# Halving and reordering the weight loads of a two-part attention kernel, with a new search of its order

## The chip, the cores and the metric

The kernel runs on one core of a Trainium2 chip. Its time is the device time of one execution in microseconds (us). TensorE (PE) does matmuls; its weight loads are shown as PEld. VectorE (DVE), ScalarE (ACT) and GpSimd (POOL) work on tiles. SyncE (SP) and POOL issue most DMAs here, ACT a few. Each engine works through its own queue in order.

## The reference, cut to what matters

Two attentions over the same input `x` (2048 tokens of 576 numbers, bfloat16) are mixed by a gate.

```python
g = sigmoid((x * gate_w).sum(-1))
# A: recurrent over 64 segments of 32 tokens, 32 heads of 128
for s in range(64):
    h = concat([mem, xs])                    # 8 memory rows and 32 tokens
    q, k, v = h @ Wq, h @ Wk, h @ Wv         # 576 -> 4096 each
    o = softmax(mask(q @ k.T) * scale) @ v
    o = o @ Wo                               # 4096 -> 576
    mem = o[:8]; outs.append(o[8:])
# B: plain attention over all 2048 tokens, 32 heads of 18
b = softmax(qB @ kB.T * scale) @ vB @ wo
out = g * a + (1 - g) * b
```

A's segments depend on each other through `mem`. B is independent of A until the last line.

## The kernel before

**Opening.** `x` is loaded in 16 tiles and transposed into `xT` (operations `xt`, evictions `xe`). B's projections follow: `pq` for queries and keys (five blocks of 128 columns, each in four stretches of 512 tokens; number of the kind, block, stretch), `pv` for values (two halves in 16 blocks). Their evictions `pe` and `ve` are, in order of creation, the list `beats`; the numbers in `WV_AT`, `WQ_AT`, `WK_AT` and `XT_AT` are places in it. The results go to DRAM (`ps`, `vs`) and come back by head in rings of tiles (`lq`, `lk`, `lv`). `gate` makes the gate's sums with 80 matmuls of one column.

**Weights of A.** `load_weights` loads each of `Wq`, `Wk` and `Wv` in four row chunks of 1152 KB on POOL's queue: one DMA for 128 rows (`wq_m` and so on) and two for the 16 rows left over (`wq_t`). `Wo` (`wo`) is loaded in four loads of eight heads each, also 1152 KB. `behind` paces such a load: a mark (`mk...`, a memset of one element by VectorE, after a given beat) overwrites a corner of the target, so the load on POOL must wait for it:

```python
mark = add(f"mk{name}", "DVE", 0.07, lambda e: nc.vector.memset(corner(), 0.0), [beat, *deps], prio=0.05)
op = add(name, "POOL", 0.6 * n, fn, [mark, *deps], prio=0.15, kb=kb)
```

The beats of `wo`'s loads are evictions `le0...` of the look-ahead units below.

**Look-ahead units.** The last 8 tokens of each segment are independent of `mem`'s way through the sums, so their projections are made ahead for 16 segments at once. Unit `la{q}.{kind}.{b}` (kind 0 queries, 1 keys, 2 values; b from 0 to 7) is made on TensorE in four or five parts, evicted to one of three `vl` buffers (`le`) and stored to DRAM (`ls`, into `qkd` or `vld`); `ll`, `lw` and `pl` bring it to a segment. Group q = 0 is made in the opening, the other three between the segments. `xs` stores `xT` to `xtd`.

**Recurrence.** `open` releases the opening's tiles. For each segment s, projections `Q0`, `Q1`, `K0`, `K1`, `V0`, `V1` run in quarter tiles (`pvv`), are evicted to `tm` (`eQ`, `eK`, `eV`), queries and keys are transposed by DMA on SP (`tt`) and copied to `qk` (`ct`). Then come scores `ph0`, `ph1` (tile `psh`), the exponential, sums `sm`, reciprocal `rc`, broadcast `bc`, product `nm`, values `po`, copies `co`, the output product `op` (tile `acc`), the sum `oc`, the fold `fo` (tile `pw`) and the VectorE operation `ph{s}`, which writes the new memory rows into `ht`.

**B's attention.** It is cut into 512 visits, each of four score matmuls (`sb`, `sp`), two exponentials on ScalarE and four value matmuls (`ob`). Some 48 run ahead of the first segment; the rest are tied to the segments' progress. After the last segment come B's output projection and the mix (`po` on line 1719).

**The order.** All operations are handed to `Plan`, which knows estimated durations, buffers and DMA lanes and lays out the program's instructions by a list schedule: the kernel's code order does not set it. `transfer` estimates a DMA's landing from a total rate of 300 GB/s. In gaps that it foresees on TensorE it places fillers (`warm`, matmuls of zeros into `ob`). `TURNS` holds one number for each segment and one for the opening; from it `factor` draws multipliers on the priorities of the kinds of operations, which `turn` sets at every segment's start. Another number gives another order of the same operations.

Of the kernel before, what the change touches and what calls it, by code (L numbers as in the profile page):

```python
# [54 lines left out]
]  # L55
RANK = dict(RANKS[0])
TURNS = [
    7952103, 9687964, 5516313, 4619848, 2331426, 9781478, 6767540, 9438387, 4494518, 2665133, 7827388,
    8977164, 1226615, 2691511, 8161648, 3391998, 7299576, 7499803, 5912477, 3941991, 2592632, 3325584,
    1612500, 5268309, 5100667, 9966380, 8690923, 9452778, 8585440, 8557057, 6500948, 6810124, 3017308,  # L60
    4090786, 5458572, 5723550, 5859185, 4641056, 9435998, 2730178, 9332617, 891581, 8429124, 2926893, 2493124,
    3284586, 4758985, 9564957, 2868796, 4844339, 2132632, 1055938, 8169318, 6049240, 2872012, 2408005,
    9273239, 5457756, 9293065, 1220648, 3952921, 2300746, 1937382, 5055776, 6803238,
]
FACTORS = (0.02, 0.1, 0.25, 0.4, 0.55, 0.7, 0.85, 1.0, 1.2, 1.5, 1.9, 2.4, 3.0, 4.0, 6.0, 10.0)
KNOBS = ("switch", "near", "early", "wait", "gap", "cool")
# [17 lines left out]
def kind_of(name):  # L84
    if re.match(r"(sb|ob|ex|ey)\d+\.", name):
        return name[:2]
    if re.match(r"l[ae]\d", name):
        return name[:2] + ("v" if name.split(".")[1] == "2" else "q")
    m = re.match(r"([a-zA-Z]+\d?)\.\d+(?:\.\d+)?$", name) or re.match(r"([a-zA-Z]{2})\d+$", name)
    return m.group(1) if m else "x"  # L90
# [20 lines left out]
class Plan:  # L111
# [36 lines left out]
    def transfer(self, op):  # L148

        wait, after = (0.6, 0.5) if op.end < self.CROWDED[1] else (0.9, 1.0)  # L150
        step = (op.end - op.start) / op.dmas
        for j in range(op.dmas):
            issued = op.start + (j + 1) * step
            self.moved = max(self.moved, issued + wait) + op.kb / op.dmas / 300.0
            self.lanes.append(max(self.moved + after, self.lanes[-1]))
        self.lanes = self.lanes[-self.LANES:]
        op.tail = self.lanes[-1] - op.end
# [13 lines left out]
    def add(  # L171
        self, name, engs, dur, fn, deps=(), prio=5.0, mode=None, take=(), give=(), tail=0.0, dmas=0, kb=0.0,
        use=None, pairs=4, alt=None, waits=0.0,
    ):
        op = Op(name, engs, dur, fn, deps, prio, mode, take, give, tail)
        op.dmas, op.kb = dmas, kb
        op.pairs, op.alt, op.form, op.waits = pairs, alt, mode, waits
        op.kind = self.kinds.setdefault(kind_of(name), len(self.kinds))
        op.use = self.ARRAY.get(mode) if use is None else use
        op.seq = len(self.ops)  # L180
        op.slots = {}
        self.ops.append(op)
        return op
# [19 lines left out]
    def run(self):  # L203
# [20 lines left out]
        while len(order) < n + extra:  # L224
# [3 lines left out]
            for e in free:  # L228
                b = best[e]
# [5 lines left out]
            est, op = best[pick]  # L235
            if pick == "PE" and open_ and self.warm is not None:
                for m in ("col", "full"):
# [6 lines left out]
                    w = Op("warm", "PE", self.WARM, self.warm[m], [], 9.0, m, (), (), 0.0)  # L244
# [39 lines left out]
            if op.dmas and pick == "ACT" and op.prio < 0.05:  # L284
                op.tail = 2.0
            elif op.kb and pick == "POOL":
                self.moved = max(self.moved, op.end + 0.6) + op.kb / 300.0
                op.tail = 2.2 + op.kb / 250.0 if op.dmas else self.moved + 1.0 - op.end
            elif op.dmas:
                self.transfer(op)  # L290
                dirty.add("SP")
# [85 lines left out]
def kernel(  # L377
# [15 lines left out]
    nc = tc.nc  # L393
    P = nc.NUM_PARTITIONS
# [16 lines left out]
    NF = 4  # L411
    RW = Dm // NF
    TR = RW - P
    TL = NF * TR
    HD = H * Dh
    WB = HD // NF
# [14 lines left out]
    plan = Plan()  # L431
# [30 lines left out]
    for jj in range(2):  # L462
        nc.vector.memset(bsel[64 * jj:64 * jj + 64, jj:jj + 1], 1.0)
    nc.gpsimd.affine_select(
        out=veil[0:64, M:L], in_=veil[0:64, M:L], pattern=[[1, seg]],
# [3 lines left out]
        out=veil[0:64, 0:M], in_=veil[0:64, 0:M], pattern=[[0, M]],  # L469
        compare_op=ALU.is_gt, fill=-30000.0, base=L, channel_multiplier=-1,  # L470
    )
    for j in range(4):
# [3 lines left out]
        out=keep[:, NF + 1:NF + 2], in0=keep[:, NF:NF + 1], scalar1=-1.0, scalar2=1.0, op0=ALU.mult, op1=ALU.add  # L476
# [49 lines left out]
    def bank(shape, dt, name, k=0):  # L526
        return ps_a.tile(shape, dt, name=name, tag=f"pb{plan.slot('pb', k)}")
# [42 lines left out]
    def rows(t, c):  # L570
        return t[RW * c:RW * c + P, :]
# [84 lines left out]

    wbl = [*wbt, *wbq.values()]
    beats, weight_loads, paced = [], {}, []
    WV_AT, WQ_AT, WK_AT = (1, 5, 25, 29), (33, 37, 41, 45), (49, 53, 57, 60)
    XT_AT = (63, 64, 66, 67)  # L660

    def behind(name, beat, corner, n, fn, deps, kb):

        mark = add(f"mk{name}", "DVE", 0.07, lambda e: nc.vector.memset(corner(), 0.0), [beat, *deps], prio=0.05)
        op = add(name, "POOL", 0.6 * n, fn, [mark, *deps], prio=0.15, kb=kb)
        paced.append(op)
        return op

    def load_weights(w, src, name, at):
        w2 = src.rearrange("d h e -> d (h e)")  # L670
        weight_loads[name] = []
        for c in range(NF):
            def load_w(e, c=c):
                nc.gpsimd.dma_start(
                    out=w[0][:, :, c, :], in_=rows(w2, c).rearrange("p (b f) -> p b f", f=WB)
                )
                for two in range(2):
                    o = 32 * c + TR * two
                    nc.gpsimd.dma_start(
                        out=w[1][o:o + TR, :],  # L680
                        in_=w2[RW * c + P:RW * c + RW, two * (HD // 2):(two + 1) * (HD // 2)],
                    )

            weight_loads[name].append(behind(f"{name}{c}", at[c], lambda c=c: w[0][0:1, 0, c, 0:1], 3, load_w, [], 1152))

    def load_gw(e):
        for c in range(NF):
# [7 lines left out]
    def store_xt(q):  # L695
# [4 lines left out]

        deps = [beats[XT_AT[q]]] + [o for n in range(4 * q, 4 * q + 4) for o in xdone[n][:1]]
        return add(f"xs{q}", "SP", 0.4, fn, deps, prio=3.0, dmas=1, kb=655)
# [212 lines left out]
    for gq in range(GB * NQC):  # L915
# [3 lines left out]
        for kb in range(NKB):  # L919
            c = 4 * g + kb // KC  # L920
            o = (kb % KC) * P
# [176 lines left out]
    opened = {}  # L1098
# [21 lines left out]

    opening = add("open", "POOL", 4.0, open_rest, b_work + early + paced, prio=0.5)

    wo_loads = []
    for q in range(4):
        def load_wo(e, q=q):
            nc.gpsimd.dma_start(out=opened["wo"][:, 8 * q:8 * q + 8, :], in_=A_Wo[8 * q:8 * q + 8].rearrange("h e d -> e h d"))

        wo_loads.append(behind(
            f"wo{q}", [o for o in plan.ops if o.name.startswith("le0.")][2 + 5 * q],
            lambda q=q: opened["wo"][0:1, 8 * q, 0:1], 1, load_wo, [opening], 1152,  # L1130
        ))

    def load_m0(e):
        m0 = opened["ot"][:, :, :].rearrange("p h t -> p (h t)")[:, 0:Dm]
# [47 lines left out]
    def out_pieces(name, o_of, t0, hf, state, first, last, prio, deps, take, halves=None, wide=False):  # L1182
        def piece(lo):
            def fn(e):
                if state.get("acc") is None:
                    state["acc"] = bank([P, 2 * RW if wide else RW], FP32, "acc")
                acc, o, wo = state["acc"], o_of(), opened["wo"]
                for s_ in range(lo, lo + 4):
                    slot = hf * 16 + s_
                    h = (s_ // 4) * 8 + 4 * hf + s_ % 4  # L1190
                    for j in range(2 if wide else 4):
                        q = 2 * (s_ % 2) + j if wide else j
                        n, d = (2 * RW, 2 * RW * j) if wide else (RW, RW * SL[j])
                        nc.tensor.matmul(  # L1194
                            acc[32 * q:32 * q + 32, :], lhsT=o[:, slot, t0:t0 + CT], rhs=wo[:, h, d:d + n],
                            start=(first and s_ == (s_ % 2 if wide else 0)), stop=(last and s_ == (14 + s_ % 2 if wide else 15)),
                            tile_position=(0, 32 * q), skip_group_check=True,
                        )
            return fn

        op = None
        for k in range(4):
            d = [*(deps if op is None else [op]), *(halves[k // 2] if halves else ())]
            op = add(
                f"{name}{k}", "PE", 0.243 if wide else 4 * 0.0625, piece(4 * k), d, prio=prio, mode="col",
                take=take if k == 0 else (), pairs=8 if wide else 16,
            )
            state.setdefault("op0", op)
        return op
# [32 lines left out]
    for s in range(n_seg):  # L1242
# [122 lines left out]
        ots = []  # L1365
        mids = {}
        for hf in range(2):
# [141 lines left out]
            for jj in range(2):  # L1509
# [10 lines left out]
                ))  # L1520
            acc_state = {}
            mids[hf] = out_pieces(
                f"op{hf}.{s}.", lambda: opened["ot"], 0, hf, acc_state, True, True, RANK[f"op{hf}"],
                wo_loads, ("pb",), [[o] for o in ots[2 * hf:2 * hf + 2]], wide=not hf,
            )
            if hf == 0:
                first_half = acc_state
# [223 lines left out]
    ahead, behind = RANK["ahead"], RANK["behind"]  # L1751
    share = (NB - ahead - behind) / n_seg
    for i, vi in enumerate(order):
        if i >= ahead:
            k = min(int(8 * (i - ahead) / share), 8 * n_seg - 1)
# [40 lines left out]
```

## Time and profile before

| what | value |
|---|---|
| median of 3 runs | 1420.84 us (1417.83 to 1429.57) |
| the profiled execution's own time | 1421.8 us |
| its span | 1420.0 us, 74484 instructions |
| PE busy | 1345.2 us (95%) |
| ACT busy | 1091.4 us (77%) |
| DVE busy | 848.2 us (60%) |
| POOL busy | 535.4 us (38%) |
| moved by DMA | 130.73 MB, mean 92 GB/s |

The span is what the profiler saw from the first instruction to the last. Busy time is summed by engine; a busy TensorE is one with matmuls in flight, with modelled ends. A line such as L1312 is a line of the kernel; where a helper makes the call (L540, L538), the tile's name tells which operation it is. In brackets after a timeline row stands the idle time of the engine before it and what ended it. The granted clock is the share of full clock that TensorE got.

### The profile page before, as it was taken

Reading aid. Unit: us, or ns where it says so; the run is one execution under the profiler, and the core shown is the slowest. Engines: PE = TensorE matmul, PEld = TensorE weight load, DVE = VectorE, ACT = ScalarE, POOL = GpSimd, SP = SyncE. Lnnn points to the kernel's source line nnn. Section 1 sums busy time; section 2 is a strip of 40 time slices with the busy share of each in tenths; the row PEclk is TensorE's granted clock in tenths of the full one; section 3 lists DMA queues with packets and bytes.
Section 4 is the critical chain, followed back from the end, with each engine's and each line's share of the span. In section 5 each row is a group of like instructions: output and inputs, shape, how many; then the busy total and the mean of one; then the engine's idle time right before and its main releaser. Section 6 shows DMA issues by size and latency. Waiting matters only on the chain. (4 is left out here: it accounts for less than half of the span.)

```text
span 1420.0 us, 74484 instructions
## 1 busy us (share of the span) xinstructions
PE 1345.2 (95%) x33172; PEld 720.4 (51%) x33184; DVE 848.2 (60%) x2019; ACT 1091.4 (77%) x1277; POOL 535.4 (38%) x1162
## 2 busy tenths in 40 slices
PE   7999899999999999999999999999999999999998
PEld 4555344555554545555555544555554545444545
DVE  4443466665565566656666655656656665665566
ACT  3477688888887787887887888787778788887884
POOL 7352154334532346332543425333354324521310
PEclk9999999999999999999999999999999999999999
DMA  8787544333433344333433334333335333333335
GB/s 251 253 314 220 131 87 75 64 68 69 82 62 64 60 79 76 76 61 65 85 67 70 69 66 76 68 62 69 65 80 89 60 54 59 72 56 53 56 81 169
DMA packets 343997, 130.73 MB, mean 92 GB/s; under 512 B 296495, under 2 KB 330023, under 8 KB 343675
## 3 DMA queue, kind: packets, MB, share of 16 engines
q1 hardware_dynamic: 315155, 80.47, 29.2%
q0 software_dynamic: 26368, 43.31, 11.4%
q8 instruction: 259, 4.24, 1.3%
q10 hardware_dynamic: 2152, 2.19, 0.5%
q14 instruction: 63, 0.52, 0.1%
HBM read 52.74 MB, written 31.12 MB: 59 GB/s over the span
## 5 line engine op out<-in xcount | busy, mean ns | idle before, releaser
L941 ACT ACTIVATE etb<-sb 128x1536 bf16<-128x1536 f32 x512 | 743.5, 1452 | 227.5 <-PE sp L932 153.0
L540 DVE CAST tm<-pvv 128x512 bf16<-128x512 f32 x358 | 246.3, 688 | 230.3 <-PE pvv L1312 228.3
L945 ACT ACTIVATE etb<-sp 128x512 bf16<-128x512 f32 x512 | 305.0, 596 | 4.8 <-PE sp L932 4.8
L1312 PEld LDWEIGHTS <-ht 128*32 128x32 bf16 x7680 | 202.8, 96 | 196.2 <-issue 21.6
L932 PE MATMUL sb<-qch,kch 32*128 32x512 bf16 x1536 | 201.8, 386 | 3.2 <-ACT etb L941 1.8
L932 PE MATMUL sp<-qch,kch 32*128 32x512 bf16 x512 | 197.6, 386 | 7.6 <-DVE vl L540 5.8
L955 PE MATMUL ob<-etb,vch 128*32 128x512 bf16 x2048 | 201.9, 387 | 0.3 <-issue 0.3
L1194 PE MATMUL acc<-wo,ot 128*32 128x288 bf16 (+1 forms) x6144 | 165.7, 248 | 7.3 <-issue 3.6
L1312 PE MATMUL pvv<-wq_m,ht 128*32 128x512 bf16 x2048 | 142.1, 380 | 3.9 <-DVE ht L1559 1.5
L1312 PE MATMUL pvv<-wv_m,ht 128*32 128x512 bf16 x2048 | 141.7, 380 | 0.3 <-DVE tm L540 0.2
L1312 PE MATMUL pvv<-wk_m,ht 128*32 128x512 bf16 x2048 | 140.5, 380 | 0.1
L1194 PEld LDWEIGHTS <-ot 128*32 128x32 bf16 x6144 | 112.7, 97 | 47.0 <-DVE ot L540 17.7
L540 DVE CAST ot<-pso 128x320 bf16<-128x320 f32 x200 | 91.6, 484 | 58.3 <-PE pso L1500 57.3
L932 PEld LDWEIGHTS <-kch 32*128 32x128 bf16 x2048 | 54.5, 91 | 137.0 <-issue 121.7
L1411 DVE COPY qk<-tt 128x512 bf16<-128x512 bf16 x256 | 79.9, 314 | 54.5 <-DMA tt<-tm 51.2
L1261 POOL COPY ht<-xg 128x96 bf16<-128x96 bf16 x64 | 17.7, 277 | 236.8 <-PE pvv L1312 230.5
L955 PEld LDWEIGHTS <-vch 128*32 128x32 bf16 x2048 | 53.6, 94 | 73.5 <-issue 62.5
L851 POOL DMA_DIRECT2D qch<-qtd x120 | 61.7, 521 | 68.3 <-PE sp L932 64.6
L851 POOL DMA_DIRECT2D otd<-stage x124 | 62.8, 513 | 65.0 <-DVE stage L998 38.6
L540 DVE CAST vl<-pv 128x512 bf16<-128x512 f32 x84 | 57.2, 685 | 38.8 <-PE pv L1025 21.8
L1489 DVE TENSOR_TENSOR et<-et,prb 128x320 bf16<-128x320 bf16 x128 | 61.6, 484 | 28.0 <-PE prb L1478 23.1
L1444 ACT ACTIVATE et<-psh 128x320 bf16<-128x320 f32 x128 | 56.6, 445 | 27.0 <-PE psh L1434 25.7
(161 smaller groups left out, 1968.1 us busy)
## 6 DMA issues: line engine op xcount, KB each, us to landing
xl<-qkd SPq DMA_DIRECT2D x64, 128.0 KB
v_sb<-tm SPq DMA_DIRECT2D x256, 32.0 KB
qkd<-vl POOLq DMA_DIRECT2D x48, 128.0 KB, 2.5
wo<-in_A_Wo_dram POOLq DMA_DIRECT2D x4, 1152.0 KB, 10.9
vgd<-vt SPq DMA_DIRECT2D x32, 128.0 KB
wv_m<-in_A_Wv_dram POOLq DMA_DIRECT2D x4, 1024.0 KB
wq_m<-in_A_Wq_dram POOLq DMA_DIRECT2D x4, 1024.0 KB, 9.2
wk_m<-in_A_Wk_dram POOLq DMA_DIRECT2D x4, 1024.0 KB
```

The source lines that it names most:

```text
L540: nc.vector.tensor_copy(out=out_of(), in_=in_of())
L851: dma(out=rows_, in_=pads) if out else dma(out=pads, in_=rows_)
L932: nc.tensor.matmul(sb[:, j, :] if j < 3 else sp[:, :], lhsT=kc[r, o:o + P], rhs=qt_[r, :], start=True, stop=True, tile_position=(32 * j, 0),)
L941: nc.scalar.activation(out=etb[:, 0:3, :], in_=box["sb", gq, kb][:, :, :], func=ACT.Exp, scale=scale_b)
L945: nc.scalar.activation(out=etb[:, 3, :], in_=box["sp", gq, kb][:, :], func=ACT.Exp, scale=scale_b)
L955: nc.tensor.matmul(ob[32 * j:32 * j + 32, :], lhsT=vc[:, o + 32 * j:o + 32 * j + 32], rhs=etb[:, j, :], start=(kb == 0), stop=(kb == NKB - ...
L1194: nc.tensor.matmul(acc[32 * q:32 * q + 32, :], lhsT=o[:, slot, t0:t0 + CT], rhs=wo[:, h, d:d + n], start=(first and s_ == (s_ % 2 if wide ...
L1261: nc.gpsimd.tensor_copy(out=ht[:, 0:NF, M:CT], in_=xg[:, 0:NF, t])
L1312: nc.tensor.matmul(pv[32 * j:32 * j + 32, :], lhsT=ht[:, cc, :], rhs=rw, start=(c == 0), stop=(c == NF), tile_position=(0, 32 * j), skip_g ...
L1411: eng.tensor_copy(out=opened["qk"][:, hf, a, 0:16 * L].rearrange("p (j i t) -> p j i t", i=4, t=L)[:, :, :, 0:CT], in_=box["tt", s, a, hf] ...
L1444: nc.scalar.activation(out=opened["et", hf][:, :], in_=box["psh", s, hf][:, :], func=ACT.Exp, scale=scale_a)
L1489: nc.vector.tensor_tensor(out=et[:, :], in0=et[:, :], in1=box["prb", s, hf][:, :], op=ALU.mult)
```

## The change

Four things change together.

1. The projection weights of A are loaded in 24 loads of 576 KB rather than 12 of 1152 KB: each row chunk in two halves of the columns, with one DMA for the 128 rows and one for the tail. Queries' weights come first, then keys', then values'; the beats are new.
2. The output weights are loaded in eight loads of four heads (576 KB), each with its own beat among the look-ahead evictions, in the order 0, 2, 4, 6, 1, 3, 5, 7. In segment 0 each quarter of an output product depends on the one load that it reads; before, the first quarter depended on all four. Later segments name no load.
3. The planner counts 290 GB/s for transfers that end before its 150 us, 300 after.
4. `TURNS` is replaced; one number of 65 is kept.

```diff
 TURNS = [
-    7952103, 9687964, 5516313, 4619848, 2331426, 9781478, 6767540, 9438387, 4494518, 2665133, 7827388,
...
+    7101990, 5457611, 1094547, 6271972, 3376618, 6037905, 9008482, 5524051, 5984833, 1797702, 7693482,
...
-            self.moved = max(self.moved, issued + wait) + op.kb / op.dmas / 300.0
+            self.moved = max(self.moved, issued + wait) + op.kb / op.dmas / (290.0 if op.end < 150.0 else 300.0)
...
-    WV_AT, WQ_AT, WK_AT = (1, 5, 25, 29), (33, 37, 41, 45), (49, 53, 57, 60)
+    WQ_AT, WK_AT = (13, 16, 19, 22, 26, 28, 30, 32), (34, 36, 38, 40, 43, 46, 49, 51)
+    WV_AT = (53, 55, 57, 59, 61, 62, 65, 66)
     XT_AT = (63, 64, 66, 67)
+    WO_AT = (10, 12, 14, 16, 18, 20, 21, 22)
...
         for c in range(NF):
-            def load_w(e, c=c):
-                nc.gpsimd.dma_start(
-                    out=w[0][:, :, c, :], in_=rows(w2, c).rearrange("p (b f) -> p b f", f=WB)
-                )
-                for two in range(2):
+            for two in range(2):
+                def load_w(e, c=c, two=two):
+                    half = slice(two * NF // 2, (two + 1) * NF // 2)
+                    cols = slice(two * (HD // 2), (two + 1) * (HD // 2))
+                    nc.gpsimd.dma_start(
+                        out=w[0][:, half, c, :], in_=rows(w2, c)[:, cols].rearrange("p (b f) -> p b f", f=WB)
+                    )
                     o = 32 * c + TR * two
...
+                    nc.gpsimd.dma_start(out=w[1][o:o + TR, :], in_=w2[RW * c + P:RW * c + RW, cols])
+
+                weight_loads[name].append(behind(
+                    f"{name}{c}{two}", at[2 * c + two], lambda c=c, two=two: w[0][0:1, two * NF // 2, c, 0:1], 2, load_w, [], 576,
+                ))
...
-    for q in range(4):
-        def load_wo(e, q=q):
-            nc.gpsimd.dma_start(out=opened["wo"][:, 8 * q:8 * q + 8, :], in_=A_Wo[8 * q:8 * q + 8].rearrange("h e d -> e h d"))
...
+    for k, at in zip((0, 2, 4, 6, 1, 3, 5, 7), WO_AT):
+        def load_wo(e, k=k):
+            nc.gpsimd.dma_start(out=opened["wo"][:, 4 * k:4 * k + 4, :], in_=A_Wo[4 * k:4 * k + 4].rearrange("h e d -> e h d"))
...
+            if name.endswith(".0."):
+                d.append(wo_loads[2 * k + hf])
```

## The prediction

> **What bounds the kernel.** I read the whole span first, in forty slices, then tables by stretch, then the waits of the opening, and last TensorE's own timeline where a stretch looked poor.
>
> The forty slices of the page:
>
> ```profile
> PE   7999899999999999999999999999999999999998
> PEclk9999999999999999999999999999999999999999
> GB/s 251 253 314 220 131 87 75 64 68 69 82 62 64 60 79 76 76 61 65 85 67 70 69 66 76 68 62 69 65 80 89 60 54 59 72 56 53 56 81 169
> ```
>
> TensorE is 90% busy or more nearly everywhere. The DMA engines are loaded only in the first four slices (to 142 us), where all projection weights, their intermediates and most of the output weights move. The change's loads all lie there. The table by stretch (length, busy us of PE, PEld, DVE, ACT, POOL, then granted clock, DMA share, GB/s) gives the poor places:
>
> ```profile
> 28.00:36.00 8.00, 5.89 (x34) 2.93 (x32) 2.91 (x6) 2.30 (x3) 8.00 (x40) 0.79 0.84 301
> 52.00:60.00 8.00, 7.49 (x32) 2.45 (x31) 1.99 (x6) 2.75 (x4) 1.78 (x3) 0.57 0.76 237
> 143.00:150.00 7.00, 1.25 (x10) 0.17 (x8) 1.58 (x3) 2.00 (x3) 0.00 (x0) 0.83 1.01 222
> 150.00:156.00 6.00, 5.78 (x30) 1.64 (x35) 1.75 (x3) 2.54 (x3) 0.00 (x0) 0.63 0.27 90
> 173.00:1369.00 1196.00, 1146.35 (x30802) 613.41 (x30798) 737.03 (x1758) 963.07 (x1135) 461.88 (x982) 1.00 0.37 68
> ```
>
> The last row is the recurrence. Its state write `ph` tells the pace:
>
> ```profile
> L1559 DVE TENSOR_TENSOR ht<-pw,keep x63: 144/207/209, 173.2 to 1368.5; 128x48 bf16<-128x48 f32 x63
> ```
>
> (1368.5 - 173.2) / 62 = 19.28 us per segment, TensorE 96% busy. There the limit is TensorE shared between the chain of a segment and attention visits; no weight load touches it. So the change can save in the first 173 us, and it can shift the 1196 us only through the new order. The opening's lost time is in these waits (who waited for whom from 0 to 175 us: total, times, longest) and TensorE rows of the timeline (start, length, and in brackets the idle time before it):
>
> ```profile
> DVE vl L540 <- DMA qkd<-vl: 10.9, 5, 4.9
> ...
> DVE qk L1411 <- DMA tt<-tm: 8.5, 1, 8.5
> ...
> DVE xn L540 <- DMA qtd<-xn: 4.6, 1, 4.6
> ```
>
> ```profile
> 27.34 0.39 PE L932 MATMUL sp<-qch,kch 32*128 32x512 bf16 x1 [1.08 <-DMA kch<-ktd]
> ...
> 31.03 0.86 PE L773 MATMUL pvb<-wb,xT 128*128 128x288 bf16 x5 [2.11 <-DVE xn L540]
> ...
> 32.36 3.28 PE L773 MATMUL pvb<-wb,xT 128*128 128x288 bf16 x15
> ...
> 118.93 0.38 PE L1025 MATMUL pv<-xL,wk_m 128*128 128x128 bf16 x4 [0.98 <-DVE vl L540]
> ...
> 149.42 0.58 PE L932 MATMUL sp<-qch,kch 32*128 32x512 bf16 x1 [5.75 <-DVE vl L540]
> ```
>
> Four stalls follow. **A** (27 to 36 us): 1.08 + 2.11 us idle, because a store from `xn` lands late behind two value-weight loads (issued at 22.4 and 26.0 us); then 15 `pvb` matmuls take 3.28 us where 50 later take 6.12, that is 1.84 for 15, a loss of 1.4, and 0.4 more on the rows around: 5.0 us. **B** (52 to 58): a slow clock after the 80 one-column matmuls of `gate`; the change keeps that instruction. **C** (115 to 125): the query and key units wait for free `vl` buffers behind the `xtd` and `qkd` stores: 7 full fillers of 0.21 (1.5), 0.98 and 0.69 idle, 3.2 us. **D** (143 to 155): 5.75 us idle. It comes from DVE's in-order queue: `ct10.0` waits 8.5 us for a transpose (139.6 to 148.1) that shares the DMA engines with an output-weight load of 1152 KB (issued at 139.7) and the `xl` loads, where the transpose before it took 4.1 us; and the `vl` evictions behind `ct10.0` hold TensorE's banks. From 149.4 to 154.3 matmuls then start 0.43 apart, not 0.21; the listed work would take 2.8 of those 4.8 us: 2.0 more. D is 7.75 us.
>
> **The change, part by part.**
>
> Halved loads: 12 pairs of marks and loads become 24, with two DMAs each (a main part and one tail), so 36 DMAs become 48; four output loads become eight. VectorE: 16 more memsets of 0.06 us, 1 us beside 40% idle time. POOL: 0.81 us per 1024 KB issue and 0.49 per tail before; with 0.65 for a half (an estimate, between 0.81 and the 0.51 of the 18 KB issues) 24 x 1.14 - 12 x 1.79 = 5.9 us, spread over 80 us in which POOL is under half busy. On the strict POOL queue each load waits for its mark. Behind them now stand `gw`, the 16 `xl` gathers, `lq2`, `lk4`, `lv4`, `lq3`. In the changed kernel's instruction order their first users (`gate`, `la0`, visit `sb2.0` or later) come well after the mark concerned, so I cost it at nothing; without that cover it is one round of two projections and a visit per late mark, 2.9 us (94.5 to 97.4). `wo4` to `wo7` now hold back `lq4` and `pl0`, but `pl0` needs the last key store anyway.
>
> [...] The row: between 80 and 90 us, with 1024 KB loads, 64 KB tails and 128 KB stores mixed, the table by stretch shows 393 GB/s at a DMA share of 1.04. [...]
>
> Order of the weights: queries' first half is now marked by `pe110`, and two halves (1152 KB) are in flight before the store that A waited for, where 2304 KB were. A shrinks between 0 and 5.0; half the bytes, I take -3.0. [...]
>
> C: the value weights now end with mark beat 66, four `xtd` stores (640 KB each) follow, and the order shows 15 fillers between `la0.0.5` and `la0.2.0`, for the same shortage of `vl` buffers. 15 x 0.21 = 3.2 is certain; what lies beyond is 0 to 4, I take 0.8, as C itself had more idle than fillers but only by 1.7. Against C's 3.2: +0.8.
>
> D: all eight value units and their `vld` stores are now ahead of the last ten query and key units, and the first transposes come after the last unit, so no `vl` eviction stands behind a `ct` on DVE. D goes: -7.75. Late next is the first transpose, with the last two output loads (1152 KB) issued shortly before it. The row for such a load beside a transpose is 8.5 - 4.1 = 4.4 us more, and the other bound is 0, if both have landed: each is 1.9 us at 300 GB/s, and two units and a projection (some 6 us) stand between. I take 2.0, nearer to the landed case. Each piece of segment 0's output product now waits for its own load; six projections (30 groups of 0.216, 6.5 us) and the softmax stand ahead of it, so that wait costs nothing.
>
> New order elsewhere: changes of TensorE tile mode go from 1291 to 1305, +14 at 0.12 us (the gaps between `pq`, `ob` and `sb` at 94.3 to 95.1 us): +1.7. All fillers: 145 before, 152 after; the opening has 10 more, so the rest has 3 fewer: -0.6. Recurrence, segments 1 to 62: mode changes 1121 and 1118, chain and visits the same instructions. The ring of look-ahead units runs 34 more blocks as 5 full matmuls rather than 20 quarter ones, 0.28 against 0.30 us: nothing. The trace does not show the new order; I bound it at 0.15 us per segment either way (9 us) and take 0.
>
> Sum: -3.0 + 0.8 - 7.75 + 2.0 + 1.7 - 0.6 = -6.9 us against the profiled execution's 1421.8 us (span 1420.0, 1.8 around it): 1414.9. The median of the runs is 1.0 lower than that execution, so **1414 us**.
>
> **The rivals.** *The order gains too* (chance 0.2): the same sum with 0.15 us per segment less, 1405 us. For it: 51.2 us of waits for transposes in the whole trace. Against: as many fillers and mode changes as before. *The stall only moves* (0.2): fillers plus a wait for the value weights or for `vld` stores behind 2560 KB of `xtd`, some 7 us at C; 1421 us. For it: the late value loads and the 15 fillers. Against: queries' and keys' weights are in long before. *The new order lengthens the recurrence* (0.13): each segment waits 0.25 us more, for example for a transpose behind other work of the SP queue; 62 x 0.25 = 15.5, so 1429 to 1430 us. It outweighs the opening from 6.9 / 62 = 0.11 us per segment. For it: the chain of a segment passes two or three transposes of some 4 us. Against: the same operations in nearly the same places.
>
> **How the numbers follow.** My own case has 0.47, its range 1406 to 1421. The ends of the transposed bounds and the rivals stretch 8 in 10 to 1400 to 1429. One per cent, 14 us, is about what a measurement of this kernel tells from no change: faster than 1406.6 takes most of the first rival and some of my case (0.23); slower than 1435 takes part of the last (0.09); the rest is 0.68.
>
> **What would show it.** After: `ph` of segment 0 near 166 us with about 54 visits done (48 now), no PE gap over 3 us before it, fillers at about 105 to 112 us, and a pace of 19.1 to 19.3 us per segment (six visits fewer remain). A later first `ph`, or a pace off by over 0.15 us, makes the sum wrong; DMA rates under 300 GB/s at 70 to 100 us would speak for the fixed cost.

## The result and the profile after

| kernel | median (runs) | ratio to before, 95% interval |
|---|---|---|
| before, beside it | 1421.72 us (1417.58 to 1429.57, 10) | 1 |
| after | 1413.9 us (1411.07 to 1418.83, 10) | 0.9941 [0.9922, 0.996] |
| after, repeated later as a control | 1411.76 us (1408.07 to 1418.79, 6) | 0.9918 [0.989, 0.9946] |

The change saves about 8 us by the first comparison (10 by the second), which is 0.6 to 0.8%. The forecast was 1414. The profiled executions were slower than the medians: 1416.22 us for after (span 1414.1) and 1418.79 us for the control, against 1421.8 for before. A single profile therefore shows only 3.0 to 5.6 of the 8 to 10 us, and the account below is one of those executions.

The same three rows of the page, in forty slices, of the kernel after:

```profile
PE   7999999999999999999999999999999999999998
PEclk9999999999999999999999999999999999999999
GB/s 229 273 319 223 148 84 68 60 70 75 75 66 72 61 76 73 70 65 69 84 66 72 59 68 78 72 60 70 63 101 68 61 56 56 66 61 54 57 64 187
```

The 8 in TensorE's fifth slice (142 to 178 us) is now a 9; nothing else can be seen at this grain. The table by stretch (length, then busy us of PE, PEld, DVE, ACT, POOL, then granted clock, DMA share, GB/s) of the kernel after:

```profile
28.00:36.00 8.00, 6.63 (x54) 4.15 (x53) 3.44 (x9) 4.28 (x5) 4.23 (x17) 1.00 0.64 192
52.00:60.00 8.00, 7.90 (x45) 2.79 (x42) 3.37 (x7) 5.10 (x6) 2.51 (x4) 1.00 1.01 309
143.00:150.00 7.00, 7.00 (x112) 3.75 (x109) 3.06 (x7) 6.26 (x8) 1.66 (x3) 1.00 0.95 300
150.00:156.00 6.00, 4.99 (x83) 2.13 (x80) 1.78 (x4) 5.07 (x6) 2.04 (x4) 1.00 1.39 133
```

The third row is what matters: from 143 to 150 us TensorE goes from 1.25 busy us to all 7. The fourth row holds what comes late next: a full us is missing, at a DMA share over 1 for only 133 GB/s: the median of the DMA packets that start there is 64 bytes, against 1024 in the third row. The waits from 0 to 175 us and four rows of the timeline of after say who waits there:

```profile
DVE vl L540 <- DMA qkd<-vl: 8.4, 3, 6.5
...
DVE xn L540 <- DMA qtd<-xn: 3.5, 2, 1.9
...
DVE qk L1416 <- DMA tt<-tm: 3.4, 2, 3.2
```

```profile
29.81 0.65 PE L935 MATMUL sb<-qch,kch 32*128 32x512 bf16 x3 [1.37 <-DMA kch<-ktd]
...
111.05 1.90 PE L905 MATMUL ob<-unit,nil 128*32 128x512 bf16 x32
...
156.85 0.37 PE L935 MATMUL sp<-qch,kch 32*128 32x512 bf16 x1 [1.87 <-DVE tm L540]
...
158.83 1.50 PE L905 MATMUL ob<-unit,nil 128*32 128x512 bf16 x12
```

The wait for a transpose is 3.2 us at most (it was 8.5), and no gap of TensorE between 20 us and the first `ph` passes 2 us (it was 5.75; a wait of 3.5 to 3.8 us for the first input tile, at 4 us, stands in all three profiles). The third row is the end of the chain that the prediction named as late next: the copy of the first transpose waits until 155.31, evictions on DVE wait behind it, and TensorE behind those. The fourth row is the cost of that gap afterwards: 12 matmuls of a filler take 1.50 us, while the same 12 took 0.82 in the control. Last the pace, from the memory write `ph` (first of after, then of the control):

```profile
L1564 DVE TENSOR_TENSOR ht<-pw,keep x63: 169/207/209, 169.8 to 1362.7; 128x48 bf16<-128x48 f32 x63
```

```profile
L1564 DVE TENSOR_TENSOR ht<-pw,keep x63: 168/208/209, 169.1 to 1365.0; 128x48 bf16<-128x48 f32 x63
```

(1362.7 - 169.8) / 62 = 19.24 us per segment, and 19.29 in the control; it was 19.28. The first of these writes, called the first fold from here on, comes 3.4 and 4.1 us earlier. To see what was won, the span is cut at the first and the last `ph`; the first two stretches of before and of after:

```profile
0.00:173.20 173.20, 154.86 (x1678) 80.36 (x1688) 78.27 (x187) 101.43 (x111) 70.60 (x176) 0.95 0.77 239
173.20:1368.50 1195.30, 1145.65 (x30782) 613.21 (x30780) 736.82 (x1757) 962.37 (x1135) 461.68 (x981) 1.00 0.37 68
```

```profile
0.00:169.80 169.80, 158.52 (x1757) 81.51 (x1761) 79.18 (x205) 114.22 (x124) 87.86 (x202) 0.98 0.84 244
169.80:1362.70 1192.90, 1146.08 (x30173) 612.77 (x30166) 726.04 (x1747) 955.79 (x1136) 451.17 (x964) 1.00 0.37 68
```

TensorE's idle time in the opening falls from 173.2 - 154.86 = 18.3 us to 169.8 - 158.52 = 11.3, so 7.1 less, and the clock rises from 0.95 to 0.98. Of the time gained, 3.7 us went into more work ahead of the fold (54 visits done, not 48; eight more fillers). The recurrence's busy time stayed where it was, and what lies behind the last `ph` too (51.5 us before, 51.4 after).

### The profile page after: what moved, and what is told of

It is laid out like the page before. It is cut to its first block, busy times and chain, and to the rows that moved or that the text cites. A ratio compares the mean times of both kernels' runs of the same rounds, so it can differ in the third digit from the quotient of the medians.

```text
span 1414.1 us, 73462 instructions
## 1 busy us (share of the span) xinstructions
PE 1349.3 (95%) x32651; PEld 720.9 (51%) x32651; DVE 839.4 (59%) x2027; ACT 1097.6 (78%) x1291; POOL 542.2 (38%) x1172
## 5 line engine op out<-in xcount | busy, mean ns | idle before, releaser
L540 DVE CAST tm<-pvv 128x512 bf16<-128x512 f32 x354 | 243.3, 688 | 233.4 <-PE pvv L1317 229.4
L540 DVE CAST vl<-pv 128x512 bf16<-128x512 f32 x78 | 53.2, 684 | 35.1 <-PE pv L1028 21.1
```

The costliest lines, as they stand in the source:

```text
L540: nc.vector.tensor_copy(out=out_of(), in_=in_of())
```

## The experiments

Each new kernel was run beside the kernel before, and the ratios are to that. "First fold" and "recurrence" (first to last `ph`) are from its one profile.

| run | median us | ratio [95%] | first fold | recurrence |
|---|---|---|---|---|
| old order's numbers, new loads | 1438.31 | 1.0124 [1.0096, 1.0151] | 172.4 | 1212.9 |
| new order's numbers, old loads | 1435.72 | 1.0103 [1.0075, 1.0132] | 178.3 | 1208.9 |
| after, planner at 300 GB/s | 1420.91 | 1.0004 [0.9986, 1.0022] | 168.6 | 1202.9 |
| after, whole main loads | 1416.78 | 0.9966 [0.9949, 0.9982] | 174.0 | 1190.4 |
| before, one output load earlier | 1419.38 | 0.9971 [0.9952, 0.9991] | 169.8 | 1197.4 |
| after, four output loads | 1417.33 | 0.9959 [0.994, 0.9977] | 175.4 | 1188.6 |
| after, no search | 1523.59 | 1.0703 [1.0676, 1.0731] | 170.6 | 1292.7 |
| before, no search | 1519.04 | 1.0674 [1.0645, 1.0702] | 177.1 | 1282.5 |
| after, last output load earlier | 1413.66 | 0.9943 [0.9924, 0.9963] | 169.9 | 1190.2 |
| after, last output load later | 1419.09 | 0.9969 [0.995, 0.9988] | 176.8 | 1190.8 |

**Loads and order apart.** The kernel after with the old numbers of the order, and the kernel before with the new ones:

```diff
 # after, with before's numbers
 TURNS = [
-    7101990, 5457611, 1094547, ...
+    7952103, 9687964, 5516313, ...
```

> New loads, beats and the 290 GB/s, with the old numbers of TURNS: asks how much the loads bring alone. The built order has 213 fillers on TensorE, where the changed kernel has 152 and the kernel before 145, and 51 visits before the first fold. Theory 'the loads carry it' (the stall at the first transposes goes with them): first fold at 172 us or earlier, pace 19.2 to 19.4 us per segment, 1414 to 1418 us. Theory 'the order must be searched for these loads': some 60 fillers more, 0.21 us each, stand for gaps of 12 us or more: 1424 to 1432 us.

```diff
 # before, with after's numbers
 TURNS = [
-    7952103, 9687964, 5516313, ...
+    7101990, 5457611, 1094547, ...
```

> Old loads and rate with the new TURNS: asks how much the searched order brings alone. The built order has 194 fillers, 49 more than before. Theory 'the order carries it': 1412 to 1417 us, pace 19.24 us or less. Theory 'loads and order only fit together': fillers for some 10 us more than before, 1425 to 1434 us, and a stall of several us behind the large loads stays in the first 173 us.

Measured: 1438.31 and 1435.72 us, each about 1% slower than before. Neither part is worth anything without the other; both times lie above even the range expected for that case (1432 and 1434 us at most). The loss is in the recurrence, 17.6 and 13.6 us longer than before's 1195.3, where none of the changed loads runs. The first also lays out 61 more fillers than after (213 to 152); at 0.21 us that is 13 us of the 24 that it lies above after, so about as much again is lost beside the fillers. The reading that fits both, and the next run too, is that the numbers of `TURNS` fit one planned time line: shift its opening by a few us, and they are arbitrary numbers for the segments that follow.

**The planner's rate.** The kernel after with one number changed back in both places:

```diff
-... + op.kb / op.dmas / (290.0 if op.end < 150.0 else 300.0)
+... + op.kb / op.dmas / 300.0
-... + op.kb / (290.0 if op.end < 150.0 else 300.0)
+... + op.kb / 300.0
```

> The changed kernel with the planner's 300 GB/s throughout: loads the same, the order replanned from an estimate 3% higher in the first 150 us. 182 fillers against 152. If the constant is only a label on the plan: 1412 to 1416 us. If the numbers of TURNS fit one planned timeline only: 30 fillers more, 6 us, 1417 to 1423 us, lost in the segments and not in the opening, which has 4 fillers fewer.

Measured: 1420.91 us, no better than before. The opening is even 1.2 us shorter than after's, and the recurrence 10 us longer (30 more fillers in the order, 182 to 152). Whether 290 is the truer estimate this run can't say; the rate is part of the time line that the numbers were searched for.

**Whole loads in after's own order.** Every instruction of TensorE, VectorE and ScalarE keeps its place. The first of each two loads of a row chunk moves only its 64 KB tail, and the second the whole main part of 1024 KB:

```diff
-nc.gpsimd.dma_start(
-    out=w[0][:, half, c, :], in_=rows(w2, c)[:, cols].rearrange("p (b f) -> p b f", f=WB)
-)
+if two:
+    nc.gpsimd.dma_start(
+        out=w[0][:, :, c, :], in_=rows(w2, c).rearrange("p (b f) -> p b f", f=WB)
+    )
```

> The changed kernel's order, instruction for instruction on TensorE, with each row chunk's main part loaded in one DMA of 1024 KB at the second half's mark (the first half's op loads only its 64 KB tail; nothing is left out): 12 main loads and not 24. [...] A third: late whole loads delay stores, a stall of 2 to 5 us comes back in the opening: 1416 to 1419 us.

Measured: 1416.78 us. The 12 whole loads are some 3 us slower than the 24 halves (by the ratios; the intervals just overlap), which is in the range of the third case. The DMA rate is much the same: 331 GB/s from 70 to 80 us, 314 from 80 to 90 and 297 from 90 to 100, where after has 332, 300 and 291. The waits from 0 to 175 us and two rows of the timeline of this kernel:

```profile
DVE xn L540 <- DMA qtd<-xn: 11.7, 5, 5.4
...
DVE vl L540 <- DMA qkd<-vl: 11.5, 4, 7.4
```

```profile
29.14 2.18 PE L737 MATMUL pq<-xT,wb 128*128 128x512 bf16 x5 [2.01 <-DVE xn L540]
...
35.23 0.65 PE L935 MATMUL sb<-qch,kch 32*128 32x512 bf16 x3 [2.71 <-DMA kch<-ktd]
```

With a whole load in flight, the store from `xn` is late again and stall A is back, with gaps of 2.01 and 2.71 us where after has one of 1.37. Aligned operation by operation with after, this profile is 4 us behind at 28 us, 7 at 33, 5.5 at 60 and 4.2 at the first fold. What goes with the size of a load is the longest wait for that store: 5.4 us here, 4.6 before and 4.5 with the new numbers and old loads, but 2.4 at most in the five profiles of after's order with halves. That A as a whole hangs on it is not shown: the kernel before with one output load earlier (next) has A without that wait, A's slow clock came back in two of those five as well (see A below), and in these two and here the copy of an early input tile had waited 2.5 or 2.6 us for its load, where the other three of the five waited 1.8.

**Stall D in before's own order.** Only bytes move: the first output load keeps head 0 in its place beside the transpose, and its other seven heads go with a load some 12 us earlier (issued at 128.1 us).

```diff
-nc.gpsimd.dma_start(out=opened["wo"][:, 8 * q:8 * q + 8, :], in_=A_Wo[8 * q:8 * q + 8]...)
+lo, hi = (0, 1) if q == 0 else (8 * q, 8 * q + 8)
+nc.gpsimd.dma_start(out=opened["wo"][:, lo:hi, :], in_=A_Wo[lo:hi]...)
+if q == 3:
+    nc.gpsimd.dma_start(out=opened["wo"][:, 1:8, :], in_=A_Wo[1:8]...)
```

> The kernel before with its order untouched; of the first output-weight load (heads 0 to 7, issued at 139.7 us beside the transpose that took 8.5 us) only head 0 stays in its place, and the other seven heads are loaded in the slot of another output-weight load, at about 126 us. All output weights are loaded. Theory (stall D comes from that load beside the transpose): the longest wait for a transpose before 175 us falls from 8.5 to 4 or 5 us, TensorE's 5.75 us wait at 149 us to under 2, the first fold comes 4 to 6 us earlier, and the time is 1415 to 1417 us against 1421. Rival (the gathers of the look-ahead's small rows, which share the DMA engines with it too, make the transpose late): the wait stays over 7 us, the stall over 5, and the time at 1420 to 1422.

Measured: 1419.38 us, 0.9971 [0.9952, 0.9991], so about 4 us of 1422 saved, between 1 and 7. Waits from 0 to 175 us, then two rows of the timeline of this kernel:

```profile
DVE qk L1414 <- DMA tt<-tm: 4.9, 2, 2.7
```

```profile
145.02 0.29 DVE L1414 COPY qk<-tt 128x512 bf16<-128x512 bf16 x1 [2.21 <-DMA tt<-tm]
...
146.45 0.37 PE L932 MATMUL sp<-qch,kch 32*128 32x512 bf16 x1 [2.37 <-DVE vl L540]
```

The transpose that took 8.5 us now takes under 4 (issued at 141.1, copied at 145.0), TensorE's gap falls from 5.75 to 2.37 us, the half clock behind it lasts 3.4 us rather than 6.8, and the first fold comes 3.4 us earlier. Aligned at 141 us, where this kernel is 0.4 us behind, it gains 3.8. So the load caused about half of D's 7.75 us and most of the long wait; the gathers alone, which are still there, don't cause that. The gap that is left, 2.4 us, is still one of `vl` evictions behind `ct` on DVE. The median came out above the expected 1415 to 1417: the first fold gained less than 4 to 6 us, and in this one profile the recurrence is 2.1 us longer.

**The late transposes in after's order.** Three kernels move output-weight bytes away from the first transposes, with all other instructions in place. The first makes four loads of 1152 KB in the first four slots:

```diff
-nc.gpsimd.dma_start(out=opened["wo"][:, 4 * k:4 * k + 4, :], ...)
+k % 2 or nc.gpsimd.dma_start(out=opened["wo"][:, 4 * k:4 * k + 8, :], ...)
```

> The kernel after with its order untouched; its eight output-weight loads are four of 1152 KB, in the slots of the first four (the last at about 135 us), and the slots at 142, 144 and 146 us, shortly before the first transposes, are empty. All output weights are loaded. Theory (the output loads delay those transposes, as the prediction had it): the first transposes land about 3 us earlier (152 rather than 155 us), TensorE's 1.87 us wait for them and the slow clock behind it go, the first fold comes at 166 to 168 us rather than 169.8, and the time is 1410 to 1412 us against 1414. Rival (the look-ahead gathers delay them, or the larger output loads now delay the value stores): the transposes land at 155 us or later, and the time is 1414 to 1417.

Measured: 1417.33 us, the rival's number. Aligned with after, its profile is 5.3 us behind at 129 us, 4.2 of it from before 60 us, where the two kernels are the same; 8.0 behind at 138 us, after 1.66 us of waiting for a value store and 3.28 for a query and key store; 7.7 at 150 us; 4.4 behind at the first transposed copy; and 5.6 at the first fold. The first transposed copy of after, then of this kernel:

```profile
155.31 0.29 DVE L1416 COPY qk<-tt 128x512 bf16<-128x512 bf16 x1 [3.17 <-DMA tt<-tm]
```

```profile
159.74 0.32 DVE L1416 COPY qk<-tt 128x512 bf16<-128x512 bf16 x1
```

The transposes were issued at 148.7 and 156.4 us, so it took 6.6 and 3.4 us to the copy. Both theories hold, then: the copy gains 3.3 us when these loads are gone from in front of the transposes, and 2.1 of that is left at the first fold (TensorE then waits 1.30 us for the reciprocal `rc`, tile `rq`); and the stores lose more than that when the loads stand among them (from 4.2 to 7.7 us behind).

Beside the next two the kernel after ran once more, unchanged, as a control.

> The kernel after, unchanged, as a control beside the next two and as a second profiled execution. The same ratio to before as in its own comparison, 0.992 to 0.996. If stalls A, B and the wait for the first transposes differ from the first profile of it by less than 1 us, the point by point reading of that profile stands; if the stretch up to 60 us differs by several us (as two kernels with the same orders did), differences of one or two microseconds there can't be read from single profiles.

Measured: 1411.76 us, 0.9918, just under the expected 0.992. The wait for the first transposes and the rows of the four poor stretches differ by under 1 us from the first profile of it, as a row of its timeline shows at the late transposes, with the filler behind it:

```profile
156.57 0.37 PE L935 MATMUL sp<-qch,kch 32*128 32x512 bf16 x1 [1.18 <-DVE tm L540]
...
157.75 0.82 PE L905 MATMUL ob<-unit,nil 128*32 128x512 bf16 x12
```

So the reading of the kernel after stands, while the kernel with four loads has shown that the stretch up to 60 us can also run 4 us late.

The second moves one load only, to about 135 us:

```diff
+n = {6: 8, 7: 0}.get(k, 4)
-nc.gpsimd.dma_start(out=opened["wo"][:, 4 * k:4 * k + 4, :], ...)
+n and nc.gpsimd.dma_start(out=opened["wo"][:, 4 * k:4 * k + n, :], ...)
```

> The kernel after with its order untouched; of the eight output-weight loads the last (heads 28 to 31, issued at 145.9 us) is loaded together with heads 24 to 27 at about 135 us, and its own slot is empty. Theory (any bytes taken from shortly before the first transposes are worth their share of the late-next stall, and one load is little enough not to delay the value stores): the first transposes land 1 us earlier relative to the work before them, time 1 us below the control. Rival (the DMA engines are full from 125 to 150 us, so the bytes only delay a store instead): within 1 us of the control or above it.

Measured: 1413.66 us, ratio 0.9943 against the control's 0.9918; no gain. The rival had the DMA engines full from 125 to 150 us: after's DMA share there is 0.80, with 0.39 from 130 to 135 us and 0.90 to 0.96 from 135 on, where the load went. A `vl` eviction waits 3.80 us for a store until 143.9, and at 150 us this kernel is 1.8 us behind after. The transposed copy then comes 1.5 us earlier than in after (153.85), again a gain of 3.3; by the first fold, at 169.9, 1.7 of it is left, just what the wait for the store had cost.

The third moves it behind the transposes, on SP's queue:

```diff
-nc.gpsimd.dma_start(out=opened["wo"][:, 4 * k:4 * k + 4, :], ...)
+k == 7 or nc.gpsimd.dma_start(out=opened["wo"][:, 4 * k:4 * k + 4, :], ...)
...
 # after the gather xl of segment 2
+if s == 2:
+    dma(out=opened["wo"][:, 28:32, :], in_=A_Wo[28:32]...)
```

> The kernel after with its order untouched but for one transfer: heads 28 to 31 of the output weights are loaded from SP's queue behind the third gather of the look-ahead, at about 161 us, where the DMA engines are under half busy, and their slot at 145.9 us is empty. Theory (bytes moved behind the transposes relieve them, and the load lands by 167 us, before the output product of segment 0 needs it): 1 to 2 us below the control. Rival (the load lands after 168 us, or holds up the transfers of the first visits on SP's queue): TensorE waits for it ahead of the first fold, and the time is 0 to 3 us above the control.

Measured: 1419.09 us, 0.9969: 7 us above the control, the rival's way but more than its 0 to 3 us, and not by its first mechanism. TensorE and SP's queue of this kernel ahead of the first fold:

```profile
165.48 1.11 SPq L1282 DMA_DIRECT2D wo<-in_A_Wo_dram  x1
166.65 1.15 SPq L1358 DMA_DIRECT2D v_sb<-tm  x2
```

```profile
171.09 0.19 PE L1507 MATMUL pso<-et,v_sb 64*128 64x40 bf16 x1 [1.63 <-DMA v_sb<-tm]
172.24 0.31 PE L1507 MATMUL pso<-et,v_sb 64*128 64x40 bf16 x7 [0.96 <-DMA v_sb<-tm]
```

The load was issued at 165.5 us, not 161, and just ahead of the two transfers that bring segment 0's values. TensorE waits 1.63 + 0.96 us for those and for no weight. The first fold, at 176.8, is 7.0 us later than in after. This execution has stall A as well and runs 4.4 us behind after at 60 us and 4.2 at 150; at the first transposed copy it is only 0.9 behind, the same gain of 3.3. Some 2 us are lost at 165 us, before the load was issued, mainly to a wait of 1.75 us for `rq` that the kernel with the earlier load has too. The two gaps are 2.6, and a clock of 0.50 from 171.5 to 174.9 us behind them makes up the rest.

**Without a search.** Both kernels with a plain planner:

```diff
-TURNS = [ ... ]
+TURNS = [0] * 65
```

> The kernel after with its searched order taken away: all TURNS are 0, so that the planner chooses without them. Nothing else changes. 344 fillers in place of 152. By the fillers alone (192 of 0.21 us) 40 us more than after, 1454; if each filler stands for as much again lost beside it, as in the run with new loads and old turns (61 fillers, 24 us), 75 us more, 1490. Theory (the order carries most of what the loads can give or take): 1450 to 1490. Rival (the search is worth little, the new loads do the work): under 1430.

> The kernel before with all TURNS 0: no searched order and the old loads. 373 fillers in place of 145. By the fillers 48 us more than before, 1469; with as much again beside them 1511. Against the run of after without turns: if the new loads are worth something by themselves, this one is more than 12 us slower than that (31 more fillers are 6.5 to 12 us); if the order alone carries the change, within 12 us of it or faster.

Measured: 1523.59 and 1519.04 us; the intervals overlap. Both lie above their expected ranges: with 192 more fillers than after the first is 110 us slower, 0.57 for each and not 0.21 to 0.4. The two can't be told apart, so without a search the new loads are worth nothing that shows in the time. The opening and the recurrence of after without a search:

```profile
0.00:170.60 170.60, 155.69 (x1790) 83.32 (x1799) 76.78 (x199) 103.05 (x114) 84.79 (x195) 0.99 0.81 243
170.60:1463.30 1292.70, 1195.16 (x33390) 636.51 (x33386) 704.73 (x1681) 989.86 (x1203) 470.56 (x990) 0.99 0.33 63
```

Against after, the opening is 0.8 us longer and the recurrence 99.8: 49 us of more busy time and 51 of more idle time. The search earns its 100 us between the segments. The new loads shorten the opening with or without it: 170.6 against 177.1 us without a search, 169.8 against 178.3 with the new numbers, though with the old ones only 172.4 against 173.2; but the visits done by then differ by two or three, and what they win the recurrence may take back (1292.7 against 1282.5).

No run tests the old loads with a fresh search of their own. How much of the 8 us comes from the loads, and how much from one more search, therefore stays open.

## Why the prediction was right, and where it was not

**The sum.** -6.9 us was predicted against the profiled execution; the profiled executions of after show -5.6 and -3.0, the medians -8 and -10. The sign, the size and the place hold. What lies between the profiles and the medians, 2 to 7 us, can't be put to a place for certain, since no profile caught a median execution of after; the recurrence is the likeliest (see the new order below). That the median fell on the forecast to 0.1 us is in part luck: A gave less than its term, and the recurrence probably more.

**D, -7.75: right, and half of it shown.** The gap and its slow clock are gone. Taken away alone in the old order, the load accounts for about 4 us; that the rest is the order of `vl` and `ct`, as the prediction had it, was not tried apart.

**Late next, +2.0: right.** In after the chain costs a gap of 1.87 us and about 0.7 of slow clock at the fillers, and some more around it; in the control one gap of 1.18 and one of 1.00 us at full clock. That is between 2 and 3.5. That it comes from the last output loads is shown by the three kernels that move them: in each the first copy comes 3.3 us earlier relative to the work before it, and in two 2.1 and 1.7 us of that are left at the first fold.

**A, -3.0: mis-sized, and not steady.** After keeps one gap of 1.37 and one of 1.10 us at full clock, so 2.5 of 5.0 were saved. But two of the five profiles with after's loads in this stretch (the kernel with four output loads and the one with the late load) have a slow clock there again, 0.86 and 0.72 from 28 to 36 us, with the same instructions and transfers, and run 4.2 and 4.4 us behind after at 60 us, more than A had saved. The idle time itself is much the same in all five, 2.5 to 2.8 us against 3.2 before; so what the change saves steadily here is under 1 us, and the clock decides the rest. In both slow ones the copy of an input tile in the first 15 us waits 0.8 us longer for its load than in after. That the late input is the cause was not tested. (The 6.12 us that the step counts for 50 matmuls are 6.30 in the trace; the loss of 1.4 stays.)

**B, 0: right, but the two profiles differ.** The slow stretch only came earlier: from 44 us ten `pq` matmuls take 3.92 us rather than 2.33. It lasts 3.4 us where before had 6.8 (52 to 59 us), which is some 2 us less lost. That is not the change: the kernel before with one output load earlier, with the same instructions up to there, has 3.4 us too.

**C, +0.8: slightly high.** The 15 fillers came about where they were expected, 109 to 114 us, and take 3.2 to 3.5 us; nothing was lost beyond them. VectorE waits 6.5 us for a `vl` buffer, but TensorE is 99.5% busy from 110 to 120 us.

**Mode changes, +1.7, and fillers, -0.6: not sized by any run.** The counts are about right: the trace has 17 more changes, all in the opening, and fillers 8 more in the opening, 3 fewer in the recurrence and 2 more behind it.

**The halved loads, 0: right.** The sum has no term for the 16 splits. No run shows a fixed cost of a load, which the last sentence of the prediction names. What the runs show: after moves 332 GB/s from 70 to 80 us, 300 from 80 to 90 and 291 from 90 to 100, so 308 over the three, with the last one alone under the 300 set there; with the halves merged it is 331, 314 and 297, and the kernel was no faster (1416.78 us). Behind the larger loads a store of 128 KB from `xn` was waited for 5.4 us, behind the halves 1.9.

**The new order, 0 in the recurrence: right in total, wrong in its picture.** The step took the order to be a neutral reshuffling with 0.15 us per segment either way. The recurrence did stay in the two profiles of after (-2.4 and +0.6 us). The four other kernels with exactly after's order have 1188.6 to 1190.8 us, however, and the two profiles with before's order 1195.3 and 1197.4: with the same instructions the recurrence scatters by 7 us, and its mean over six is some 5 us below before's (three of the four have a later first fold, which may play a part). So a gain of a few us there is likely and not shown.

But the runs with loads and order apart show that a planned order that doesn't fit the kernel loses 14 to 18 us there, and one number of the planner 10: the order is not a term beside the others, it is the condition for all of them. The step also left out that six more visits ahead of the first segment take TensorE's time there. So the test "first `ph` near 166" failed (169.8, 169.1) while the idle time removed, 7.1 us (5.3 in the control), is about the 6.9 forecast. Why the recurrence of after has the same busy time with six visits and 609 matmuls fewer (510 of these from 34 look-ahead blocks made in 5 full matmuls rather than 20 quarter ones) stays open.

**The rivals.** That the order gains too would have shown as a recurrence shorter by 9 us: no profile shows so much, though the mean of six has half of it. That the stall only moves to C: no, C cost what its fillers cost. That the new order lengthens the recurrence: not this order, but all five that were not searched for exactly their loads and rate did just that.

## What to carry to other kernels

When a queue that works in order waits for a small transfer, look for the large load that was issued just before or beside it; the price of that load is what stands behind the wait, not its bytes: before waited 8.5 us for a transpose beside a load of 1152 KB, and TensorE 5.75 us behind that; with one head of the eight left there it was under 4 and 2.37 us. Moving bytes may only choose who waits: with one load of 576 KB moved away from the transposes the first copy gained 3.3 us, but a store was waited for 3.80 us (load earlier) or the values 2.6 us (load later), and neither kernel was faster. So move bytes to a place where a wait has cover, and measure. And where a searched order belongs to the kernel, judge a change only with its own search: here a small shift under an old order cost 10 to 18 us between the segments, more than the whole change brought. To know what the loads alone are worth, the old ones would need a new search too.

## What the runs showed that was not expected

**In before and after a slow clock came behind 1.78 us or more of idle time, summed over a stretch of 3.41 us.** In these two traces, from the first record of the clock (11.1 and 10.4 us) on, it is either 1.00 or 0.50 and changes only at multiples of 3.41 us from its other changes: apart from the ends, every slow stretch lasts 3.41 or 6.83 us. So these two profiles can be cut into stretches of 3.41 us in which the clock is constant. Behind a stretch at full clock came half clock where TensorE had been idle in it for 2.11, 2.27, 2.65 or all 3.41 us (before) and for 1.78, 1.87 or 2.15 us (after), and in each of the two once without idle time, behind the 80 one-column matmuls of `gate`; behind all other stretches at full clock, with 1.37 us idle at most, full clock came again. Single gaps mislead: the kernel with four output loads has gaps of 0.78, 1.06 and 0.17 us in one stretch (30.4 to 33.8 us, 2.01 in all), and 0.50 followed; after's 1.37 us stands alone in its stretch (27.5 to 30.9), and full clock followed; behind the control's 1.18 and 1.00 us (157 and 162 us) it was full too (1.00 from 156 to 173 us); after's 1.87 us (157 us) fell into one.

**The same instructions scatter by 4 us in the first 60 us.** After and the kernel with four output loads are the same up to about 125 us, and one profile ran 4.2 us behind the other at 60. A difference of a few us in the opening of two single profiles says little; alignment from a common point, and medians, decide.

**A filler can mark more than its own time.** 30, 61 and 192 more fillers than after came with 7, 24 and 110 us more: 0.23, 0.4 and 0.57 us each, against 0.21 for running one.
